# One order written out for all five engines, and three full-array visits of TensorE in a head pair

## The chip, the cores and the metric

The kernel runs on one core of a Trainium2 chip. The metric is the device time of one execution in microseconds. The engines are TensorE (PE; its weight loads are shown as PEld), VectorE (DVE), ScalarE (ACT), GpSimd (POOL) and the DMA queues, most of which SyncE (SP) issues.

## What is computed

The reference is sparse attention over key chunks, and a mixture of experts that sends each token to one expert:

```python
ub = sum(max(q * k_min_of_chunk, q * k_max_of_chunk))     # 24 chunks of 32 keys
top_chunks = argsort(where(causal, ub, -1e9))[..., -6:]
scores = scale * q @ k.T, masked to chosen chunks and to the past
attn = softmax(scores) @ v                                # 4 batches x 8 heads x 768 x 64
x = attn as 3072 tokens x 512
logits = x @ w_gate; expert = argmax(logits)              # 8 experts
out = gate * relu(x @ w1[expert]) @ w2[expert]
```

Inputs are float32; the seed of the draw is fixed.

## The kernel before

Two heads make a head pair; there are 16 pairs, `i` from 0 to 15, four to a batch (`hp = i % 4`). One pair is taken through its stages while parts of its neighbours are worked on in between: `n = i + 1` is prepared for attention, `m = i + 2` has its keys and queries transposed, `i - 1` gets its denominators and router logits, `i - 2` the last of its output rows.

The stages of a pair, with the names used below:

- k0, k1 (`k_half`): three fp32 transposes of keys each into a PSUM buffer, on DVE the maximum and minimum of each chunk (L207, L208), on ACT two scaled bf16 copies into KTE (L209, L210). q0, q1: the same for queries; DVE copies to qT (L224), ACT writes the absolute value to qA and one head's bf16 copy to QSB (L225, L227). The other head's bf16 copy of qT is made by POOL (L226); it is put into the list `late` and issued when `flush()` is called. `flush()` first empties the list `sums_` (POOL additions of router logits, L375 and L378), then `late`.
- `kse` (L233, L234): sums and differences of the chunk extremes, on DVE. `ub`: bounds by matmuls of 64 columns, evicted by ACT as ubT (L244). `select`: transposes (L249), and on DVE ubm, twelve max8 and nsel (L251, L259, L262). `mask`: nsel transposed, 64 columns wide, and copied by ACT into rows 64 to 87 of QSB (L271, L272), so that unselected chunks get a large negative score in the score matmul.
- `scores(i, u)` for seven units `u`: 0 and 1 are the first 384 queries, 2 to 6 the last 384; each is 768 score columns over the two heads (L298), an exp on ACT into P (L303), and where keys reach the diagonal a causal mask on POOL (`affine_select`, L307; one for units 0 and 5, two for 1 and 6). Units 1 and 6 consist of two parts of 256 and 128 queries, each with an exp of its own.
- `attend(i, u)`: P times V in 64-column halves, one head in each (AV, L320); after units 1 and 6 DVE copies the sum out (ot, L325); the P tiles of a query half are added up on DVE (L332) for the denominators.
- `router_steps`: `ud` multiplies the added-up P with a column of ones and the output with the gate weights, 32 columns wide (L348, L353), evicted by ACT (L356); `lgp` transposes it and divides (L361, L363, L367); `x0`, `x1` transpose the output and scale it into rows of x (L386, L388).
- `route_steps`, once per batch: `logits` and exp, `rank` (matmuls L432 to L438, then DVE), and six scatters of rows to DRAM by POOL (L454).

PSUM has three buffers for transposes and the like (`ps_m`, bufs=3), two for scores (`ps_s`), one for AV (`ps_o`). A buffer is handed on when its readers are done.

The pair loop has four groups, g0 to g3. Each runs its scores, then pieces of the neighbours' work, then `attend` for the units (0, 1), (2, 3), (4, 5), (6). The order in which PE, POOL and SP issue is the order of the program text:

```python
with tc.manual_schedule(engines={PE, POOL, SP}):
```

For DVE and ACT, a planner chooses the order from its own estimates, except in the first pair's start and from pair 15 on. On PE the order within a pair is: scores 2, 3, x1, AV 0, 1, ub (g0); scores 4, 5, rank, select, AV 2, 3, ud (g1); scores 6, k0, mask, AV 4, 5 (g2); lgp, x0, the next pair's scores 0, 1, k1, q0, q1, AV 6 (g3). Matmuls of 128 columns use the full array; AV, ub and mask are 64 columns wide, ud is 32. `flush()` is called in g0, after ub.

After the loop the last denominators and the routing of the last batch are interleaved with the first expert tiles (`up`, `down`), whose rows POOL gathers and DMA transposes (`gather`, `x_in`); the gathers of the first tiles are issued at the beginning of pair 15. A table of what each tile holds is computed by DVE in three steps during pairs 13 and 14 (`early_table`).

Of the kernel before, what the change touches and what calls it, by code (L numbers as in the profile page):

```python
# [24 lines left out]
def kernel(  # L25
# [74 lines left out]
    KS = [buf.tile([128, 64], FP32, name=f"KS{i}") for i in range(2)]  # L100
    KD = [buf.tile([128, 64], FP32, name=f"KD{i}") for i in range(2)]
# [6 lines left out]
    def consts_first():  # L108
# [12 lines left out]
        nc.gpsimd.memset(KS[0][:], 0.0)  # L121
        nc.gpsimd.memset(KD[0][:], 0.0)
# [15 lines left out]
    def consts_last():  # L138
        nc.gpsimd.memset(KS[1][:], 0.0)
        nc.gpsimd.memset(KD[1][:], 0.0)  # L140
# [7 lines left out]
        nc.sync.dma_start(out=wgb[64:128, :, E:2 * E], in_=wg_v[64:128])  # L148
        iota(rev8[:], [[-1, E]], base=E)
# [44 lines left out]
    def prep_steps(i):  # L194
        s = st[i]
        kte, qsb, ks, kd = KTE[i % 2], QSB[i % 2], KS[i % 2], KD[i % 2]
        kmx = {}

        def k_half(hf):
# [3 lines left out]
            pt = ps_m.tile([128, 384], FP32, tag="m")  # L203
            for t in range(3):
                nc.tensor.transpose(pt[:, ts(t, 128)], s["k"][:, 3 * hf + t], ident_f[:])
            pk = pt[:].rearrange("p (c w) -> p c w", w=CH)
            nc.vector.tensor_reduce(s["kmx"][:, ts(hf, 12)], pk, AX.X, ALU.max)  # L207
            nc.vector.tensor_reduce(s["kmn"][:, ts(hf, 12)], pk, AX.X, ALU.min)  # L208
            nc.scalar.activation(kte[0:64, 0, ts(hf, 384)], pt[0:64, :], AF.Copy, bias=0.0, scale=0.125)  # L209
            nc.scalar.activation(kte[0:64, 1, ts(hf, 384)], pt[64:128, :], AF.Copy, bias=0.0, scale=0.125)  # L210

        def q_t(hf):
            pt = ps_m.tile([128, 384], FP32, tag="m")
            for t in range(3):
                nc.tensor.transpose(pt[:, ts(t, 128)], s["q"][:, 3 * hf + t], ident_f[:])
            s[f"qp{hf}"] = pt

        def q_e(hf):
            pt = s[f"qp{hf}"]
            if hf == 0:  # L220
                s["qT"] = work.tile([128, 2, 384], FP32, tag="qT", name="qT")
                s["qA"] = work.tile([128, 2, 384], FP32, tag="qA", name="qA")
            qT, qA = s["qT"], s["qA"]
            nc.vector.tensor_copy(out=qT[:, hf], in_=pt[:])  # L224
            nc.scalar.activation(qA[:, hf], pt[:], AF.Abs)  # L225
            late.append(lambda: nc.gpsimd.tensor_copy(out=qsb[0:64, 0, ts(hf, 384)], in_=qT[0:64, hf]))  # L226
            nc.scalar.activation(qsb[0:64, 1, ts(hf, 384)], pt[64:128, :], AF.Copy)  # L227

        def kse():
            for hd in range(2):  # L230
                r = slice(64 * hd, 64 * hd + 64)
                c = slice(32 * hd, 32 * hd + NCH)
                nc.vector.tensor_tensor(ks[r, c], s["kmx"][r, :], s["kmn"][r, :], ALU.add)  # L233
                nc.vector.tensor_tensor(kd[r, c], s["kmx"][r, :], s["kmn"][r, :], ALU.subtract)  # L234

        def ub():
            pu = ps_m.tile([128, 384], FP32, tag="m")
            for w_, nm in ((ks, "qT"), (kd, "qA")):
                x_ = s[nm][:].rearrange("p a c -> p (a c)")
                for h in range(2):  # L240
                    nc.tensor.matmul(pu[64 * h:64 * h + 64, 0:320], lhsT=w_[:], rhs=x_[:, ds(128 + 320 * h, 320)],
                                     start=(nm == "qT"), stop=(nm == "qA"), skip_group_check=True)
            s["ubT"] = work.tile([128, 384], FP32, tag="ud", name="ubT")
            nc.scalar.activation(s["ubT"][:, 0:320], pu[:, 0:320], AF.Copy)  # L244

        def select():
            pt = ps_m.tile([128, 3, 2, 2, 32], FP32, tag="m")
            for t in range(3):
                nc.tensor.transpose(pt[:, t], s["ubT"][:, ds(c0s[t], 128)], ident_f[:])  # L249
            ubm = work.tile([128, 3, 2, 2, NCH], FP32, tag="ubm")  # L250
# [14 lines left out]
        def mask():  # L265
            pt = ps_m.tile([64, S], BF16, tag="m")
            for hf in range(2):
                for t in range(3):
                    nc.tensor.transpose(pt[:, ds(128 + 320 * hf + c0s[t], 128)],
                                        nsel[:, t, hf].rearrange("p a n -> p (a n)"), ident_b[:])  # L270
            nc.scalar.activation(qsb[64:64 + NCH, 0, 128:S], pt[0:NCH, 128:S], AF.Copy)  # L271
            nc.scalar.activation(qsb[64:64 + NCH, 1, 128:S], pt[32:32 + NCH, 128:S], AF.Copy)  # L272

        return dict(k0=lambda: k_half(0), k1=lambda: k_half(1), q0=lambda: q_t(0),
                    q1=lambda: q_t(1), q0e=lambda: q_e(0), q1e=lambda: q_e(1), kse=kse, ub=ub, select=select, mask=mask)


# [4 lines left out]
    def scores(i, u):  # L282
        kte, qsb = KTE[i % 2], QSB[i % 2]
        qb, parts = units[u]
        ps = ps_s.tile([128, 2, 512], FP32, tag="s", name="ps")
        if u in (0, 2):
            P = work.tile([128, 2, 384], FP32, tag="Pa", bufs=4, name="Pa")
        else:
            P = work.tile([128, 2, 384], FP32, tag="Pr", bufs=4, name="Pr")
        st[i][f"P{u}"] = P  # L290
        pvs = []
        for n, (kb, w, c0) in enumerate(parts):
            if len(parts) == 1:
                pv = ps[:, :, 0:w]
            else:
                pv = ps[:, n, 0:2 * w].rearrange("p (a w) -> p a w", a=2)
            for hd in range(2):
                nc.tensor.matmul(pv[:, hd, :], lhsT=kte[:, hd, ts(kb, 128)],  # L298
                                 rhs=qsb[:, hd, ds(qb * 384 + 384 - w, w)],
                                 start=True, stop=True, skip_group_check=True)  # L300
            pvs.append(pv)
# [572 lines left out]
```

## Time and profile before

| | us |
|---|---|
| three runs, median (lowest to highest) | 360.99 (360.24 to 362.16) |
| the profiled execution | 360.64 |
| its span, first to last instruction | 358.6 |
| attention, up to the last ud eviction | 248.8 |
| a plain head pair | 13.66 |

The pair's length is the distance of successive ACT evictions of ubT or ud in the timeline (for example 122.27 and 135.92). The granted TensorE clock is 0.992 of full speed over the span. In the profile, L12 is line 12 of the kernel; "a <- b" with a time in brackets is idle time before an instruction and what released it. The busy time of PE includes the modelled ends of pipelined matmuls, so a short wait can be hidden in it.

### The profile page before, as it was taken

Reading aid. Unit: us, or ns where it says so; the run is one execution under the profiler, and the core shown is the slowest. Engines: PE = TensorE matmul, PEld = TensorE weight load, DVE = VectorE, ACT = ScalarE, POOL = GpSimd, SP = SyncE. Lnnn points to the kernel's source line nnn. Section 1 sums busy time; section 2 is a strip of 40 time slices with the busy share of each in tenths; the row PEclk is TensorE's granted clock in tenths of the full one; section 3 lists DMA queues with packets and bytes.
Section 4 is the critical chain, followed back from the end, with each engine's and each line's share of the span. In section 5 each row is a group of like instructions: output and inputs, shape, how many; then the busy total and the mean of one; then the engine's idle time right before and its main releaser. Section 6 shows DMA issues by size and latency. Waiting matters only on the chain. (4 is left out here: it accounts for less than half of the span.)

```text
span 358.6 us, 7585 instructions
## 1 busy us (share of the span) xinstructions
PE 326.9 (91%) x2312; PEld 171.5 (48%) x2312; DVE 235.0 (66%) x815; ACT 231.2 (64%) x398; POOL 180.4 (50%) x296
## 2 busy tenths in 40 slices
PE   6679999999899999999999988998799999999990
PEld 5535455455455465554554545443344344444430
DVE  5799889889999898999988999846460000000000
ACT  2497797797687897867977967642344444445440
POOL 3075425445474453466534547575577665653331
PEclk9999999999999999999999999999999999999996
DMA  8619998999957999937989973476999999998851
GB/s 153 112 26 194 210 220 139 215 167 215 207 127 151 182 176 195 202 100 178 200 134 212 187 148 113 73 135 116 165 211 233 221 237 197 203 186 201 157 126 48
DMA packets 138215, 59.83 MB, mean 167 GB/s; under 512 B 122811, under 2 KB 131005, under 8 KB 138176
## 3 DMA queue, kind: packets, MB, share of 16 engines
q1 hardware_dynamic: 119072, 29.52, 45.4%
q0 software_dynamic: 17536, 29.42, 42.0%
q10 hardware_dynamic: 1568, 0.39, 0.6%
q8 instruction: 21, 0.34, 0.4%
q14 instruction: 18, 0.15, 0.2%
HBM read 56.14 MB, written 10.51 MB: 186 GB/s over the span
## 5 line engine op out<-in xcount | busy, mean ns | idle before, releaser
L332 DVE TENSOR_TENSOR Pa<-Pa,Pr 128x768 f32<-128x768 f32 (+2 forms) x112 | 81.6, 729 | 1.1
L307 POOL TENSOR_SCALAR_AFFINE_SELECT Pr<-Pr 128x256 f32<-128x256 f32 x80 | 33.5, 437 | 67.3 <-ACT Pr L303 66.1
L303 ACT ACTIVATE Pr<-ps 128x768 f32<-128x768 f32 (+2 forms) x112 | 65.0, 630 | 3.2 <-PE ps L298 2.9
L612 PE MATMUL py<-w_all,hT 128*128 x224 | 52.7, 379 | 2.7 <-DMA hT<-h__3653 1.9
L298 PE MATMUL ps<-QSB,KTE 128*128 128x384 bf16 (+2 forms) x288 | 50.4, 292 | 1.2 <-DVE QSB L711 0.2
L620 POOL DMA_INDIRECT out_dram<-y,ti_all x28 | 27.8, 993 | 30.2 <-ACT y L619 26.3
L298 PEld LDWEIGHTS <-KTE 128*128 128x128 bf16 x288 | 24.1, 97 | 27.3 <-issue 21.2
L612 PEld LDWEIGHTS <-hT 128*128 128x128 bf16 x224 | 21.8, 98 | 29.5 <-DMA hT<-h__3653 2.3
L619 ACT ACTIVATE y<-py,gt_all 128x512 f32<-128x512 f32 x27 | 18.6, 687 | 20.8 <-PE py L612 18.4
L454 POOL DMA_INDIRECT xs_dram<-xrow,sli x24 | 26.9, 1121 | 7.7 <-issue 5.0
L356 ACT ACTIVATE ud<-pu 128x384 f32<-128x384 f32 x16 | 7.9, 492 | 32.8 <-PE pu L353 30.7
L303 ACT ACTIVATE Pa<-ps 128x768 f32<-128x768 f32 x32 | 26.0, 812 | 3.8 <-PE ps L298 3.2
L601 PE MATMUL ph<-w_all,KTE 128*128 x120 | 28.4, 379 | 0.0
L169 POOL DMA_DIRECT2D w_all<-in_moe_w_dram x32 | 24.3, 760 | 0.0
L307 POOL TENSOR_SCALAR_AFFINE_SELECT Pa<-Pa 128x256 f32<-128x256 f32 x16 | 6.4, 398 | 35.3 <-ACT Pa L303 35.3
L601 PE MATMUL ph<-w_all,QSB 128*128 x96 | 22.7, 379 | 0.3 <-issue 0.3
L575 DVE TENSOR_TENSOR ti_all<-xgqA,inv_i 128x1 int32<-128x1 int32 x9 | 1.4, 159 | 29.6 <-DMA xgqA<-xs_dram,grow 29.6
L554 POOL DMA_INDIRECT xgqA<-xs_dram,grow x14 | 14.6, 1046 | 10.2 <-issue 3.3
L554 POOL DMA_INDIRECT xgqT<-xs_dram,grow x14 | 14.5, 1033 | 8.7 <-DVE gt_all L577 4.9
L325 DVE COPY ot<-po 128x384 f32<-128x384 f32 x32 | 17.7, 553 | 1.6 <-PE po L320 0.9
L575 DVE TENSOR_TENSOR ti_all<-xgqT,inv_i 128x1 int32<-128x1 int32 x8 | 1.3, 159 | 26.5 <-DMA xgqT<-xs_dram,grow 26.5
L226 POOL CAST QSB<-qT 64x384 bf16<-64x384 f32 x30 | 16.3, 551 | 4.1 <-DVE qT L224 2.8
(311 smaller groups left out, 665.0 us busy)
## 6 DMA issues: line engine op xcount, KB each, us to landing
w_all<-in_moe_w_dram POOLq DMA_DIRECT2D x32, 512.0 KB, 6.0
out_dram<-y,ti_all POOLq DMA_INDIRECT x28, 3.6
t__122<-in_k_dram SPq DMA_DIRECT2D x2, 192.0 KB, 3.5
t__125<-in_q_dram ACTq DMA_DIRECT2D x2, 192.0 KB, 4.0
t__128<-in_v_dram SPq DMA_DIRECT2D x2, 192.0 KB
t__196<-in_k_dram SPq DMA_DIRECT2D x2, 192.0 KB, 3.1
t__206<-in_q_dram SPq DMA_DIRECT2D x2, 192.0 KB, 3.8
t__209<-in_v_dram SPq DMA_DIRECT2D x2, 192.0 KB
```

Source lines behind the costliest of these rows:

```text
L169: nc.gpsimd.dma_start(out=dst, in_=src.rearrange("(c p) f -> p c f", p=128))
L298: nc.tensor.matmul(pv[:, hd, :], lhsT=kte[:, hd, ts(kb, 128)], rhs=qsb[:, hd, ds(qb * 384 + 384 - w, w)], start=True, stop=True, skip_grou ...
L303: nc.scalar.activation(P[:, :, ds(c0, w)], pv, AF.Exp)
L307: nc.gpsimd.affine_select(out=pd, in_=pd, pattern=[[0, 2], [1, 128]], compare_op=ALU.is_ge, fill=0.0, base=0, channel_multiplier=-1)
L325: nc.vector.tensor_copy(out=ot[:], in_=po[:])
L332: nc.vector.tensor_tensor(acc[:, :, 384 - w:384], acc[:, :, 384 - w:384], P[:, :, ds(c0, w)], ALU.add)
L454: d = nc.gpsimd.indirect_dma_start(out=xs_dram[:], out_offset=bass.IndirectOffsetOnAxis(ap=sli[:, u:u + 1], axis=0), in_=bst[b][f"xrow{u % ...
L554: d = nc.gpsimd.indirect_dma_start(out=xg_bufs[j % XB].bitcast(I32), out_offset=None, in_=xs_dram[:], in_offset=bass.IndirectOffsetOnAxis( ...
L601: nc.tensor.matmul(ph[:, fh, :], lhsT=xT[:, c, :], rhs=w_all[:, ds(wo + (c * F + fh * 512), 512)], start=(c == 0), stop=(c == NDC - 1), sk ...
L612: nc.tensor.matmul(py[:], lhsT=hT[:, c, :], rhs=w_all[:, ds(wo + (W1W + c * DM), DM)], start=(c == 0), stop=(c == NFC - 1))
L619: nc.scalar.activation(y[:], py[:], AF.Copy, bias=0.0, scale=fs[j]["gt"])
L620: d = nc.gpsimd.indirect_dma_start(out=out[:], out_offset=bass.IndirectOffsetOnAxis(ap=fs[j]["ti"], axis=0), in_=y[:], in_offset=None, bou ...
```

## The change

- DVE and ACT too are put in the order of the program text, everywhere. For this each helper is cut into a PE part, a DVE part and an ACT part (`k_mm`, `k_v`, `k_a`; `q_mm`, `q_v`, `q_a`; `ub`, `ub_a`; `sel_mm`, `sel_v`; `mask`, `mask_a`; `ud`, `ud_a`; `lgp_mm`, `lgp_v`; `x_mm`, `x_v`; `rank_mm`, `rank_v`; `logits`, `expo`, `gates`). `attend` becomes `av`, `add` and `o_ev`, `scores` becomes `scores` and `exps`.
- Unit 6's scores are issued at the end of g1, ahead of `ud`, as matmuls of 64 columns: two halves of the keys for each head and part. k0 moves from g2 to g1, behind the selection transposes (in pair 0 it stays in g2). On PE the order becomes: scores 2, 3, x1, AV 0, 1, ub; scores 4, 5, selection, k0, rank, AV 2, 3, scores 6, ud, mask, AV 4, 5; lgp, x0, next scores 0, 1, k1, q0, q1, AV 6.
- Units 1 and 6 keep the two heads in two PSUM banks, and one exp takes both parts.
- The additions of P tiles 5 and 6 are issued in the next pair's g0, behind `kse` of this one.
- `kse` works on both heads together: one sum, one difference, and one product with a 0/1 mask `bm`.
- `flush()` moves from g0 to g1, behind `ud_a`.
- `logits` moves from the end of g3 of the pair with hp = 0 into g0 of the pair behind it, `expo` and `gates` follow in g1; the scatters are spread otherwise. Constants that only routing needs are made in pair 2 (`consts_route`).

```diff
-    KS = [buf.tile([128, 64], FP32, name=f"KS{i}") for i in range(2)]
-    KD = [buf.tile([128, 64], FP32, name=f"KD{i}") for i in range(2)]
+    KSD = [buf.tile([128, 2, 2, 32], FP32, name=f"KSD{i}") for i in range(2)]
+    bm = buf.tile([128, 2, NCH], BF16, name="bm")
...
+        def kse():
+            kt2 = work.tile([128, 2, NCH], FP32, tag="top8", name="kt2")
+            nc.vector.tensor_tensor(kt2[:, 0], s["kmx"][:], s["kmn"][:], ALU.add)
+            nc.vector.tensor_tensor(kt2[:, 1], s["kmx"][:], s["kmn"][:], ALU.subtract)
+            nc.vector.tensor_tensor(ksd[:, :, :, 0:NCH], kt2[:].unsqueeze(2).to_broadcast([128, 2, 2, NCH]),
+                                    bm[:].unsqueeze(1).to_broadcast([128, 2, 2, NCH]), ALU.mult)
...
+    def scores(i, u, split=False):
...
+        n = 64 if split else 128
+        for kb, w, c0 in parts:
+            for hd in range(2):
+                for h in range(128 // n):
+                    nc.tensor.matmul(ps[ds(h * n, n), hd, ds(c0, w)], lhsT=kte[:, hd, ds(kb * 128 + h * n, n)],
+                                     rhs=qsb[:, hd, ds(qb * 384 + 384 - w, w)],
+                                     start=True, stop=True, skip_group_check=True)
...
+        nc.scalar.activation(P[:], ps[:, :, 0:384], AF.Exp)
...
-    spread = ((), (0,), (2, 4), (1,), (3, 5), (), (), ())
+    spread = ((), (), (0, 2, 4), (), (1, 3), (5,), (), ())
...
+    with tc.manual_schedule(engines={PE, POOL, SP, DVE, ACT}):
...
             for g in range(4):
                 if g == 0:
-                    scores(i, 2)
-                    scores(i, 3)
-                    run(rout, i - 2, "x1")
+                    for u in (2, 3):
+                        scores(i, u)
+                        exps(i, u)
+                    run(rout, i - 2, "x_mm", 1)
+                    run(rout, i - 2, "x_v", 1)
+                    if i > 0:
+                        if n < NP:
+                            add(i - 1, 5)
+                        add(i - 1, 6)
+                    av(i, 0)
+                    av(i, 1)
+                    o_ev(i, 0)
+                    if router:
+                        logits()
+                    add(i, 1)
+                    run(prep, n, "ub")
+                    run(prep, n, "ub_a")
+                    if 0 < i < NP - 1:
+                        load(n, "v")
                 elif g == 1:
...
+                    for u in (4, 5):
+                        scores(i, u)
+                        exps(i, u)
+                    run(prep, n, "sel_mm")
+                    if i > 0:
+                        run(prep, m, "k_mm", 0)
+                        run(prep, m, "k_a", 0)
+                    if router:
+                        rank_mm()
+                    run(prep, n, "sel_v")
+                    if router:
+                        expo()
+                        rank_v()
+                        gates()
+                    if i > 0:
+                        run(prep, m, "k_v", 0)
+                    av(i, 2)
+                    av(i, 3)
+                    add(i, 3)
+                    scores(i, 6, True)
+                    exps(i, 6)
+                    run(rout, i - 1, "ud")
+                    run(rout, i - 1, "ud_a")
+                    flush()
                 elif g == 2:
-                    scores(i, 6)
...
+                    run(prep, n, "mask")
+                    run(prep, n, "mask_a")
...
+                    av(i, 4)
+                    av(i, 5)
+                    add(i, 4)
+                    if m >= NP:
+                        add(i, 5)
                 else:
...
+                    run(rout, i - 1, "lgp_mm")
+                    run(rout, i - 1, "x_mm", 0)
+                    if n < NP:
+                        for u in (0, 1):
+                            scores(n, u)
+                            exps(n, u)
+                    run(rout, i - 1, "lgp_v")
+                    run(rout, i - 1, "x_v", 0)
+                    run(prep, m, "k_mm", 1)
+                    run(prep, m, "k_v", 1)
+                    run(prep, m, "k_a", 1)
+                    for hf in range(2):
+                        run(prep, m, "q_mm", hf)
+                        run(prep, m, "q_v", hf)
+                        run(prep, m, "q_a", hf)
                     if i + 3 < NP:
                         load(i + 3, "k", "q")
...
+                    av(i, 6)
+                    o_ev(i, 1)
+                    run(prep, m, "kse")
+                    if hp == 0 and b > 0:
+                        flush(sums_)
...
-                if g == 0:
-                    run(prep, i + 1, "ub")
-                    flush()
...
+                if 4 * i + g == 10:
+                    consts_route()
```

## The prediction

> **What bounds the kernel now.** First the page, for the stages: the engines' busy times and the slices of the span (tenths, 9 us each).
>
> ```profile
> PE 326.9 (91%) x2312; PEld 171.5 (48%) x2312; DVE 235.0 (66%) x815; ACT 231.2 (64%) x398; POOL 180.4 (50%) x296
> ...
> PE   6679999999899999999999988998799999999990
> ...
> DVE  5799889889999898999988999846460000000000
> ```
>
> DVE ends after slice 29: up to about 250 us the attention runs, with PE and DVE both near nine tenths. The expert stage (250 to 358.6) is not edited. Next the windows, cut at successive ubT evictions, one per head pair: a plain pair, then one with routing.
>
> ```profile
> 122.27:135.92 13.65, 13.57 (x109) 7.45 (x108) 12.61 (x39) 11.35 (x22) 6.30 (x13) 1.00 0.99 165
> 149.72:165.35 15.63, 14.21 (x119) 7.72 (x119) 14.93 (x53) 11.39 (x22) 9.90 (x15) 1.00 0.66 153
> ```
>
> Columns after the length: busy us of PE, weight loads, DVE, ACT, POOL. In a plain pair PE has no gap (13.57 of 13.65), DVE has 1.0 us, ACT 2.3, POOL half. In the routing pair DVE is full too. Last the timeline of one plain pair (110 to 126 us), for what holds PE inside that busy time and when POOL works.
>
> ```profile
> 112.42 0.95 DVE L332 TENSOR_TENSOR Pa<-Pa,Pr 128x768 f32<-128x768 f32 x1
> ...
> 113.29 0.55 DVE L207 TENSOR_REDUCE kmx<-pt 128x12 f32<-128x384 f32 x1
> 113.37 0.76 POOL L307 TENSOR_SCALAR_AFFINE_SELECT Pr<-Pr 128x256 f32<-128x256 f32 x2 [1.59 <-ACT Pr L303]
> ...
> 117.81 0.48 ACT L209 ACTIVATE KTE<-pt 64x384 bf16<-64x384 f32 x1 [0.21 <-DVE kmn L208]
> ...
> 118.92 0.70 POOL L226 CAST QSB<-qT 64x384 bf16<-64x384 f32 x1
> ...
> 121.56 0.81 ACT L303 ACTIVATE Pr<-ps 128x768 f32<-128x768 f32 x1
> ...
> 122.42 0.10 PEld L298 LDWEIGHTS <-KTE 128*128 128x128 bf16 x1 [0.30 <-issue]
> ...
> 122.75 0.31 PEld L249 LDWEIGHTS pt<-ident_f,ubT 128*128 128x128 f32 x3 [0.23 <-ACT ubT L244]
> ```
>
> Three things. (a) Unit 5's scores wait until the exp of unit 3 (121.56 to 122.37) frees its score buffer, and the selection transposes behind them start at 122.75 when ubT is there: 0.27 us of PE waiting in each pair, hidden in pipelined busy time. (b) That exp is late because ACT's chain of k copies, q copies and exps starts at 117.81, when the DVE minimum of the same PSUM bank is done. (c) The causal masks of unit 6 run beside reductions from PSUM, and the bf16 copies of qT (L226) run at 118.92, 10 us before the next unit-0 scores (129.1) read them.
>
> And one view from elsewhere, what POOL does when adds come in a row:
>
> ```profile
> 228.11 2.83 DVE L332 TENSOR_TENSOR Pa<-Pa,Pr 128x768 f32<-128x768 f32 x3
> ```
> ```profile
> 228.53 1.87 POOL L307 TENSOR_SCALAR_AFFINE_SELECT Pr<-Pr 128x256 f32<-128x256 f32 x2 [1.60 <-ACT Pr L303]
> ```
>
> Two masks took 1.87 us where the two at 113.37 took 0.76: each ended only about 0.27 us after the add that it met.
>
> **What the Trainium skill says.** "TensorEngine Tiling (Array Packing)", section Key Properties: a change of tiling mode drains TensorE. The trace agrees: three fp32 transposes take 0.35 us, and from selection to AV it is 0.48, so 0.13 for the change; from AV6 to the next scores 0.16. "PSUM — Partial Sum Buffer", section PSUM bank collisions: two engines may not read one bank at once. Here ACT did start 0.09 after kmn's end, with the data there for 1.2 us. "SBUF — State Buffer", section Who interferes with whom: a DVE instruction with two SBUF inputs contends with GpSimd's reads, the other blocks for the whole instruction. The 1.87 us agree. "TensorE: Matmul & The Clock Gate", section Weight-path perf modes: fast weight load wants 128 columns; no row here times bf16 scores with 64 columns.
>
> **The change part by part.** Times are from the start of LGP (lgp_mm's transposes) in a plain pair; before it is 114.63.
>
> *The visit removed.* Before: k0's transposes stand between UD (32 columns) and mask (64 columns), four full-array visits, nine changes of mode in a pair. After: three visits, eight changes. Before, selection to next LGP: 0.48 + 1.44 (AV2, AV3) + 1.11 (UD) + 0.34 (scores 6) + 0.43 (k0) + 1.74 (mask, AV4, AV5) = 5.54. After: 0.35 + 0.48 (k0 with its change) + 1.28 + x + 0.16 + 1.11 + 1.74 = 5.12 + x, x being unit 6 in 64-column halves. Bounds of x: 0.32 (768 columns in pairs side by side, as fp32 AV does) and 0.45 (eight loads of about 0.055, the spacing of the mask's transposes). I take 0.40: 5.52. The visit is worth 0.02 (-0.05 to +0.08).
>
> *ACT's chain to selection.* e1 is one activation, ending at 2.91 rather than 2.97, but the k copies still wait for kmn: kmx follows lgp_v and x_v without the 512 add between, 2.02 rather than 2.07. So 3.13 for 3.18. qa1 now precedes e2; two swapped items leave e3 where it was (6.93 to 6.88), so selection comes at 8.07 for 8.12. e2 ends at 6.98, just ahead of scores 4 (7.16). Gain 0.05. A plain pair without new waits: 8.07 + 5.52 = 13.59 against 13.66.
>
> *DVE.* kse from four small instructions and gaps (119.64 to 120.52, 0.88) to three, estimated 0.6. Adds 5 and 6 of the pair before (0.86 + 0.95) move behind x_v into g0; o_ev(0) then starts 7.17, add 1 ends 8.5, and selection's DVE work is ready to start at 8.65: nothing lost, and mask has 1.1 us of cover. If that cover went, mask waits for nsel. k_v(0) follows nsel at 10.74, so adds 3 and 4 come back to back from 11.67 to 13.4; LGP's DVE work is due at 14.19.
>
> *k0 earlier* (8.42 for 11.49): its load is issued at 2.0, and its last packet is about 5.7 after LGP, landing below 7.5 in every pair by the DMA records; the SP queue's order is the same. Nothing.
>
> *POOL, the step that decides.* flush() moves from g0 to behind unit 6's masks. POOL's order becomes mask 6 (two), sums (0, 1 or 2), two qT copies. Scores 6 start at 10.18, e6 runs 10.78 to 11.59, so the first mask issues at 11.66, with add 3 at 11.67. POOL alone: 0.77 + two sums 0.86 + first copy 0.50 = 2.13, at 13.79; scores 0 of the next pair, due at 13.59 + 0.79 = 14.38, would not see it. But two 768 adds (0.86 each) hold the port in that window; each lets a POOL operation out 0.27 after its end: mask 12.85, mask 13.85, sums 14.65, copy 15.15. Scores 0 wait until 15.2, 0.84 late; k1, ACT's chain and all else follow scores 0, so the pair is longer by that. With one sum 0.45, with none nothing. Bounds for two sums: 0 (POOL always first) and 1.3.
>
> Queued behind the waiting scores on PE: unit 1, k1, q0, q1, AV6; ACT and DVE wait for all of them.
>
> Sums: pair 2 has one; 3, 4, 7, 8, 11, 12 two; 6, 10, 14 one; 1, 5, 9, 13 none. Against 13.66: two sums +0.77, one +0.38, none -0.07.
>
> *Routing pairs (5, 9, 13 and the one behind).* Logits move into g0 ahead of add 1. The dependent run takes 1.42 in the tail of this trace (254.63 to 256.05), rank's 0.95, gates 0.71. Rank waits 0.36 on PE and works 0.30; mask waits for rank's PSUM buffer, 0.5: LGP 1.18 late. DVE's backlog makes k_v(1) 0.57 late, and x_v(1) waits for the row buffer that scatters 0, 2, 4 free, 0.4 to 0.6. About 2.2 over two pairs; before, 97.53 to 125.97 less two plain pairs costs 1.1 and 82.89 to 97.53 another 1.0: 2.1. Equal; pair 10 was 0.3 longer before. In 13/14 the expert table's steps (1.35, 1.0, 1.4 as dependent runs) stand in line where they were interleaved: +0.5. Bounds: -1 to +2 each.
>
> *Constants.* About 1.35 us of DVE work leaves the start (24.07 to 25.6, where o_ev is late and AV2 waits 0.42): -0.3, as k's load bounds the next step at 28.6. It reappears behind add 4 in pair 2: +0.3.
>
> *Tail.* The gathers of pair 15 and their DMAs (233.72 to the first down projection, 255.04, where PE waits 1.86) set it; add 6 behind x_v costs DVE 0.46 inside that wait. Nothing.
>
> Sum: start -0.3; pair 1 -0.1; pair 2 +0.7; six pairs of two sums +4.6; pairs 6 and 10 +0.8; routing +0.1, -0.2, +0.5. Together +6.1.
>
> The profiled execution took 360.64 (span 358.6 and 2.0 around it), 0.35 below the median 360.99. 360.64 + 6.1 = 366.7; against the median it would be 367.1.
>
> **Rivals.**
> *R1, copies in time.* POOL gets the port between the adds, or e6 comes 0.8 earlier. For it: POOL needs only 2.13 of 2.7 us. Against: 228.53. Then +6.1 loses 5.9 (6 x 0.84 + 2 x 0.45): 360.8.
> *R2, ACT's chain comes forward: faster.* If the k copies start with e1's end (2.81) and not after kmn, scores 5 and selection lose the wait of (a): selection at 7.77, 0.35 per pair; with the copies in time, thirteen pairs x 0.35 off R1: 356. It decides from 0.3 us of earlier start. Against: the 0.21 us wait at 117.81, and k_v still precedes k_a.
> *R3, DVE's backlog.* Should mask get k0's PSUM buffer instead of rank's, it waits for k_v(0), 14.6 rather than 13.0: 1.7 in each of three pairs, 372. For it: three buffers turn in order. Against: at 218.27 q1 waits for lgt, thus took the buffer freed last, not the next in turn.
>
> **How the numbers follow.** Forecast 0.53, own range 363.5 to 369.5; R1 0.20; R2 0.15; R3 0.12. Half a per cent, 1.8 us, is what a measurement here can tell from no change. Faster: R2 and a little of R1, 0.17. Same: most of R1, 0.19. Slower: the rest, 0.64. The range 358.8 to 370.8 takes in R1, the low edge leaving R2 out and the high edge most of R3.
>
> **What would show it.** A plain two-sum pair of 14.4 us with scores 0 released by POOL's copy (L226's successor), and pairs 5 and 9 free of that wait; selection at 8.0 to 8.1 after LGP; unit 6's halves within 0.32 to 0.45. Plain pairs of 13.6 make R1 right; of 13.2, R2; a mask that waits above 1 us for k_v, R3. A stall on x_v longer than 1 us, or k0 waiting for its load, would be a thing I missed.

## The result and the profile after

The changed kernel takes 422.12 us (median of 4 runs, 421.94 to 428.24) against 361.11 (360.24 to 362.16) for the kernel before on the same chip: a ratio of 1.172, 95% interval 1.163 to 1.182. The profiled execution took 428.24 us with a span of 426.5. Some executions below were disturbed and ran slower; ratios leave them out (of e8 one of four stays, so it has no interval), and the traces of e2, e8 and e14 are of disturbed executions.

The page of the changed kernel, parts 1 and 2: busy time by engine, then busy tenths and granted clock in 40 slices.

```profile
PE 345.7 (81%) x2376; PEld 182.8 (43%) x2376; DVE 240.4 (56%) x799; ACT 230.5 (54%) x366; POOL 183.5 (43%) x297
...
PE   6688968496858859695989949496978999999990
...
PEclk9999969598969897888899979799999999999997
```

TensorE has holes in most slices of the attention part, where before it had hardly any, and in the slices with holes its granted clock falls as well (mean 0.918; 0.992 before). The loss is all there: from the first to the last LGP the pairs take 273.6 us (45.1 to 318.7) where they took 206.1 (44.2 to 250.3). What lies ahead and behind is within 1 us of before.

The waits by engine and line of the changed kernel (total us, times, longest us), and one row of its DMA part (32 loads of 512 KB, median us from issue to landing; 6.0 before):

```profile
ACT KTE L218 <- PE pk L207: 44.2, 10, 5.8
PEld pk L207 <- issue: 41.8, 9, 5.9
...
DVE kmx L212 <- ACT KTE L218: 24.0, 7, 5.1
```
```profile
w_all<-in_moe_w_dram POOLq DMA_DIRECT2D x32, 512.0 KB, 8.2
```

L207 is k0's and k1's transposes. TensorE's weight load for them waits 41.8 us in 9 places, and 44.2 us of ACT are spent waiting for them. "Issue" means that no engine released them. What did is in the timeline of one pair of the changed kernel, from LGP at 146.3 on (start, duration, engine and line; in brackets the idle time before it and what ended it):

```profile
148.14 1.61 POOL L172 DMA_DIRECT2D w_all<-in_moe_w_dram  x2
148.21 1.05 SPq L193 DMA_DIRECT2D t__1823<-in_k_dram  x2
...
159.55 0.87 PE L207 MATMUL pk<-ident_f,t__1823 128*128 128x128 f32 x3 [4.72 <-DMA t__1823<-in_k_dram]
...
160.46 0.98 ACT L218 ACTIVATE KTE<-pk 64x384 bf16<-64x384 f32 x2 [4.83 <-PE pk L207]
...
163.91 0.81 ACT L325 ACTIVATE Pr<-ps 128x768 f32<-128x768 f32 x1 [2.47 <-issue]
164.79 0.76 POOL L329 TENSOR_SCALAR_AFFINE_SELECT Pr<-Pr 128x256 f32<-128x256 f32 x2 [8.68 <-ACT Pr L325]
...
167.21 1.43 POOL L172 DMA_DIRECT2D w_all<-in_moe_w_dram  x2
```

Two loads of the experts' weights (w_all, 512 KB each) are issued at 148.14, together with the load of the keys. The keys land 10.8 us after their issue; before they took 3.0 to 4.9 in every pair for which the DMA view gives a time. k0 stands in g1 now and wants them at 154.8: it waits 4.72 us, and AV 2 and 3, unit 6 and the denominators stand behind it on TensorE, unit 6's exponential behind k0's copies on ACT. So unit 6's masks are late on POOL (8.68 us of idle time), and behind these masks stand `flush()` and the next two weight loads. They go out at 167.21, once more beside the next load of keys (169.1). The lateness of one pair isn't needed for that of the next: the pair from LGP at 224.02 to LGP at 237.72 waits for no keys and takes 13.70 us, and yet the next two weight loads go out at 239.72, 0.83 us ahead of the keys, which land after 11.5 us. The place of the loads in POOL's order was enough there.

In the kernel before, the weight loads of one pair's end and the keys went out like this:

```profile
110.97 0.81 POOL L169 DMA_DIRECT2D w_all<-in_moe_w_dram  x1
...
114.08 0.79 POOL L169 DMA_DIRECT2D w_all<-in_moe_w_dram  x1
...
116.63 0.96 SPq L190 DMA_DIRECT2D t__1811<-in_k_dram  x2
```

There g1's loads stood behind unit 5's masks, and unit 6 was in g2, so the two loads were 3.1 us apart and the last of them 2.6 us ahead of the keys.

### The profile page after: what moved, and what is told of

Its sections match the earlier page's. It is cut to its first block, busy times and chain, and to the rows that moved or that the text cites. A ratio compares the mean times of both kernels' runs of the same rounds, so it can differ in the third digit from the quotient of the medians.

```text
span 426.5 us, 7566 instructions
## 1 busy us (share of the span) xinstructions
PE 345.7 (81%) x2376; PEld 182.8 (43%) x2376; DVE 240.4 (56%) x799; ACT 230.5 (54%) x366; POOL 183.5 (43%) x297
## 5 line engine op out<-in xcount | busy, mean ns | idle before, releaser
L325 ACT ACTIVATE Pr<-ps 128x768 f32<-128x768 f32 x80 | 63.5, 816 | 34.0 <-issue 14.3
L218 ACT ACTIVATE KTE<-pk 64x384 bf16<-64x384 f32 x60 | 29.1, 485 | 50.0 <-PE pk L207 44.2
L311 PE MATMUL ps<-QSB,KTE 128*128 128x384 bf16 (+4 forms) x352 | 52.6, 302 | 2.3 <-POOL QSB L243 0.8
L311 PEld LDWEIGHTS <-KTE 128*128 128x128 bf16 (+1 forms) x352 | 28.5, 113 | 33.5 <-issue 26.9
L212 DVE TENSOR_REDUCE kmx<-pk 128x12 f32<-128x384 f32 x32 | 17.8, 555 | 31.4 <-ACT KTE L218 24.0
L325 ACT ACTIVATE Pa<-ps 128x768 f32<-128x768 f32 x32 | 26.0, 812 | 15.1 <-PE ps L311 14.6
L494 POOL DMA_INDIRECT xs_dram<-xrow,sli x24 | 24.6, 1027 | 6.1 <-issue 5.3
L293 ACT ACTIVATE QSB<-pm 24x640 bf16<-24x640 bf16 x30 | 20.8, 693 | 5.8 <-PE pm L287 5.3
L421 DVE TENSOR_TENSOR xrow<-px,rec 128x384 bf16<-128x384 f32 x32 | 17.5, 550 | 6.7 <-DMA xs_dram<-xrow,sli 5.2
L594 POOL DMA_INDIRECT xgqA<-xs_dram,grow x14 | 14.6, 1042 | 14.2 <-DMA KTE<-xgqA 4.5
L370 PE MATMUL pu<-Pa,dcol 128*32 128x384 f32 x128 | 18.2, 625 | 0.3 <-DVE Pa L350 0.3
L641 PEld LDWEIGHTS <-KTE 128*128 128x128 bf16 x120 | 11.7, 98 | 15.8 <-DMA KTE<-xgqT 1.4
```

Source lines behind the costliest of these rows:

```text
L218: nc.scalar.activation(kte[0:64, hd, ts(hf, 384)], pt[64 * hd:64 * hd + 64, :], AF.Copy, bias=0.0, scale=0.125)
L293: nc.scalar.activation(qsb[64:64 + NCH, hd, 128:S], s["pm"][32 * hd:32 * hd + NCH, 128:S], AF.Copy)
L311: nc.tensor.matmul(ps[ds(h * n, n), hd, ds(c0, w)], lhsT=kte[:, hd, ds(kb * 128 + h * n, n)], rhs=qsb[:, hd, ds(qb * 384 + 384 - w, w)], s ...
L325: nc.scalar.activation(P[:], ps[:, :, 0:384], AF.Exp)
L494: d = nc.gpsimd.indirect_dma_start(out=xs_dram[:], out_offset=bass.IndirectOffsetOnAxis(ap=sli[:, u:u + 1], axis=0), in_=bst[b][f"xrow{u % ...
L641: nc.tensor.matmul(ph[:, fh, :], lhsT=xT[:, c, :], rhs=w_all[:, ds(wo + (c * F + fh * 512), 512)], start=(c == 0), stop=(c == NDC - 1), sk ...
```

## The experiments

Fourteen kernels ran. Each is compared with the kernel before on its own chip, which took 368 to 369 us on the two chips of e1 to e8 and 360 to 361 on those of the others, so ratios are given. "W" below is the theory that weight loads beside an early load of keys make the loss, "F" the forecast's (POOL's late copies), "H" that the written order of DVE and ACT itself costs it.

### POOL's queue taken apart (e1, e2, e4) and k0 back in g2 (e3)

```diff
# e1: flush() back at the end of g0
                     run(prep, n, "ub_a")
+                    flush()
...
                     run(rout, i - 1, "ud_a")
-                    flush()
# e2: the weight loads of g1 ahead of unit 6 (left out of the general loop below for g = 1)
                     for u in (4, 5):
                         scores(i, u)
                         exps(i, u)
+                    for w in range(NW):
+                        if wq[w] == 4 * i + g:
+                            load_w(w)
# e3: k0 in g2 in every pair
-                    if i > 0:
-                        run(prep, m, "k_mm", 0)
-                        run(prep, m, "k_a", 0)
...
-                    if i == 0:
-                        run(prep, m, "k_mm", 0)
+                    run(prep, m, "k_mm", 0)
# e4: the edits of e1 and e2
```

> flush() back at the end of g0, all else as after the change. Theory W (a burst of weight loads runs beside the k load, and k0, now 3 us earlier on TensorE, waits for that load): the weights of g1 still stand behind unit 6's masks on POOL and so still run into those of g2, so most of the loss stays: 395 to 418 us, k0 waiting 3 us or more in most pairs. Theory F (the forecast's: copies and sums behind unit 6's masks, under DVE's adds, hold up scores 0): about 6 us come back, 414 to 418 us, with k0's waits unchanged. Theory H (the hand order of ACT and DVE itself, k0's copies ahead of unit 6's exponential and the routing in line, is what costs): no change, 420 to 425 us.

> Only the weight loads of g1 move: issued right behind unit 5's score masks, ahead of unit 6, flush() and the loads of g2. Theory W: the burst is broken, the k load lands 4 to 6 us after its issue rather than 10 to 12, k0 waits less than 0.5 us in a plain pair, and the granted clock comes back above 0.97: 362 to 376 us. Theory F: no change beyond 2 us, 420 us. Theory H: no change beyond 5 us, 417 to 422 us.

> k0 (transposes, copies and reductions) goes to g2 behind unit 6, as pair 0 has it: the fourth full-array visit is back and the weight loads stay where the change put them. Theory W: k is wanted 3 us later, and what stood behind the waiting k0 (AV 2 and 3, unit 6, its exponential, the masks, flush and the weight loads) runs on time, so that the burst itself comes earlier: 362 to 380 us, k0 waiting under 1 us. If the burst alone delays the load by 6 us and k0's place is unimportant, 395 us or more. Theory F: 420 us. Theory H with k0's copies ahead of the exponential as the cost: the same 362 to 380 as W; with routing and the adds as the cost, above 405.

> flush() at the end of g0 and the weight loads of g1 ahead of unit 6: POOL's queue in the order that it had before the change, with the three visits and the hand order of DVE and ACT kept. Theory W: 360 to 370 us, and the difference from the kernel with the weight loads moved alone is what theory F is worth by itself, 0 to 7 us. Theory F alone: 414 to 418. Theory H: above 405 us.

| kernel | median us | ratio to before | 95% interval | ratio x 361.1 |
|---|---|---|---|---|
| changed kernel | 422.12 | 1.172 | 1.163 to 1.182 | 423.3 |
| e1, flush() in g0 | 394.76 | 1.069 | 1.059 to 1.078 | 385.9 |
| e2, weights ahead of unit 6 | 387.34 | 1.043 | 1.032 to 1.053 | 376.5 |
| e3, k0 in g2 | 390.25 | 1.058 | 1.051 to 1.066 | 382.1 |
| e4, e1 and e2 | 375.83 | 1.021 | 1.014 to 1.028 | 368.6 |

Each edit alone brings back more than half of the loss, so the parts don't add: 37 us for `flush()`, 47 for the weights, 41 for k0's place, 55 for the first two together. F alone is out: it gave 6 us for e1 and about nothing for e2 and e3. H, read as the whole loss, is out: e4 keeps the whole written order of DVE and ACT. W is borne out in kind, but its sizes were off. It expected 395 us or more of e1, which took less: `flush()` stood between the masks and the weight loads, so putting it back lets these go out earlier too, and the waits of k0's transposes for their load fall from 43.5 us to 17.8. It expected 362 to 380 us of e3, with k0 waiting under 1 us, and e3 took more: k0 still waits 3.1, 2.2 and 2.2 us in three pairs. For e2 (362 to 376) and e4 (360 to 370) the last column comes out at the edge and within, the times themselves above.

With the weights ahead, `flush()` alone is worth e2 less e4, 0.022 or 8 us (3 to 12 by the two intervals). That is near the 6 us of the forecast, but e12 below shows that only a part of it is the wait that the forecast described.

### The same two parts in the kernel before (e6, e7, e8), and DVE and ACT given back (e5)

```diff
# e6: the kernel before with the three visits
                     run(prep, i + 1, "select")
+                    if i > 0:
+                        run(prep, i + 2, "k0")
                 elif g == 2:
-                    scores(i, 6)
...
                 if g == 1:
+                    scores(i, 6, True)
                     run(rout, i - 1, "ud")
#     and g1's weight loads behind unit 5's masks, as they were
# e7: the kernel before, g1's weight loads moved to the end of g2
-                    if wq[n] == 4 * i + g:
+                    if g == 2 and wq[n] in (4 * i + 1, 4 * i + 2) or g in (0, 3) and wq[n] == 4 * i + g:
# e8: e6, with g1's weight loads left at the end of g1, behind unit 6's masks
# e5: e4, DVE and ACT in the planner's order outside the first pair and the tail
-    with tc.manual_schedule(engines={PE, POOL, SP, DVE, ACT}):
+    with tc.manual_schedule(engines={PE, POOL, SP}):
```

> The kernel of e4 (three visits; flush() and the weight loads of g1 in POOL's old order) with DVE and ACT given back to the planner outside the first pair and the tail. The kernel of e4 stood 2.1% above before; its trace lays about 3.6 us of that on the expert table's DVE steps standing in line in pairs 13 and 14 and about 1.2 us on each of three routing pairs. Theory H (the hand order of DVE and ACT is that rest): ratio 0.985 to 1.005 to before. Theory V (the visits or the split unit 6 cost it): the ratio stays at 1.015 to 1.025. If the planner does worse in plain pairs, 1.02 or more with plain pairs longer than the 13.4 us of e4.

> The kernel before with the visits alone: k0 moved to stand with selection, unit 6 in 64-column halves ahead of the denominators, g1's weight loads issued behind unit 5's masks as they were; flush() in g0 and DVE and ACT left to the planner. Theory W: the k load lands in time, so the ratio to before is 0.985 to 1.01 (the visit was put at 0.02 us a pair; e4's plain pairs of 13.4 to 13.5 us point to 0.2). If k0's early place costs by itself, without a burst: 1.03 or more, with k0 waiting over 1 us in most pairs.

> The kernel before with one thing changed: the weight loads of g1 are issued at the end of g2, right before those of g2 and so right before the next k load; k0 stays where it was, 11.5 us behind LGP. Theory W (burst and early k0 together make the loss): the k load lands 9 to 12 us after its issue, at 11 to 14 us behind LGP, and k0 waits 0 to 2 us: ratio 1.00 to 1.06. If the burst alone makes the loss: 1.12 or more. If the burst is harmless and k0's place is all: below 1.005, k landing in 4 to 5 us.

> The visits of e6 in the kernel before, with g1's weight loads left at the end of g1 and so behind unit 6's masks: early k0 and burst together, without the hand order and without flush() moved. Theory W: most of the loss of the change is here, ratio 1.07 to 1.17, k0 waiting 3 to 6 us in most pairs and TensorE's clock at half speed behind each such wait. Theory F and H, in which flush() or the hand order make the loss: below 1.03. (The kernel with flush() put back stood at 1.07 with the hand order.)

| in the kernel before | k0 where it was | k0 early, three visits |
|---|---|---|
| weight loads apart | 1 | e6: 1.016 (1.007 to 1.025) |
| weight loads together | e7: 1.004 (0.999 to 1.008) | e8: 1.065 (one run) |

e8's ratio is of one run only, 392.07 us over 368. The four cells speak for W without any written order of DVE and ACT: the burst alone costs nothing that can be told (in e7's trace k0 waits for its keys only at the start, 0.6 us, as before), early k0 and the halves of unit 6 cost 1.6%, and both together about 6.5%. In e8's trace TensorE waits for k0's keys in eleven pairs, 18.9 us in all and up to 5.9. In e7 the two weight loads still go out about 2.5 us ahead of the keys (115.11 and 117.66), in most pairs of e8 about 2 to 3 us ahead.

The 1.6% of e6 are more than W gave it (1.01 at most), and waits for keys don't make them: k0 waits 0.2 and 0.3 us, in two pairs. Its plain pairs are 13.9 us long instead of 13.66; why the planner's order does worse there was not found.

e5 stands at 1.032 (1.022 to 1.041), so the planner's order for DVE and ACT is no better than the written one as a whole, and H fails for the rest of e4 too. It is mixed in detail: e5's plain pairs take 13.9 to 14.2 us (e4's 13.5), its pairs 13 and 14 together 28.3 (e4's 30.1).

### Where the weights stand, and what is left of the forecast's own mechanism (e12)

```diff
-                    if wq[w] == 4 * i + g:
+                    if g == 3 and wq[w] in (4 * i + 1, 4 * i + 2) or g == 0 and wq[w] == 4 * i:
```

> The changed kernel, flush() where the change put it, with the weight loads of g1 and g2 still issued together, two in a row, but behind the k and q loads of g3 and not ahead of them. Theory W says that it is the weights ahead of the k load that delay it: k lands 4 to 6 us after its issue, k0 waits under 1 us in a plain pair, ratio 1.02 to 1.06 (the copies of flush() alone stood at about 11 us between e2 and e4). If two weight loads together delay k wherever they stand, k0 waits 3 us or more and the ratio is 1.10 or more.

e12 took 376.87 us, a ratio of 1.047 (1.038 to 1.056). The weight loads of g1 and g2 are still issued two in a row, but behind the keys and queries. The keys now land 3.2 to 4.2 us after their issue, by e12's DMA view (two rows of it; the weights wait instead, 9.3 us in the median):

```profile
t__1363<-in_k_dram SPq DMA_DIRECT2D x2, 192.0 KB, 4.1
...
t__1616<-in_k_dram SPq DMA_DIRECT2D x2, 192.0 KB, 3.8
```

k0 doesn't wait in any pair of its trace after the first. So it is what stands ahead of the keys that delays them, not how the weights are grouped. (The changed kernel has one such case itself: at 226.72 its two loads went out 0.8 us behind the keys, and these landed in 3.9 us.) Moving two DMA issues by a few us takes 45 us off (1.172 to 1.047), and e12 still has `flush()` where the change put it. It is therefore the kernel in which the forecast's mechanism can be seen without the waits for keys. Its timeline, around the LGP at 135.7 of a pair with two sums:

```profile
133.90 1.49 POOL L329 TENSOR_SCALAR_AFFINE_SELECT Pr<-Pr 128x256 f32<-128x256 f32 x2 [1.78 <-ACT Pr L325]
...
134.17 2.02 DVE L350 TENSOR_TENSOR Pa<-Pa,Pr 128x768 f32<-128x768 f32 x2
...
135.36 1.55 POOL L407 TENSOR_TENSOR lg<-lg,lgt 128x96 f32<-128x96 f32 x2
...
136.85 0.94 POOL L243 CAST QSB<-qT 64x384 bf16<-64x384 f32 x2
...
137.40 0.82 PE L311 MATMUL ps<-QSB,KTE 128*128 128x384 bf16 x6 [0.81 <-POOL QSB L243]
```

Two masks take 1.49 us beside DVE's adds instead of 0.76, the sums 1.55, the first bf16 copy of qT ends about 137.3, and scores 0 have waited 0.81 us for it. The waits say 5.1 us in 7 places for scores on that copy: about 0.8 in each of five pairs with two sums, 0.7 in the sixth, and 0.3 in pair 2. Plain pairs with two sums are 14.2 to 14.4 us long, those with none or one 13.6 to 13.7. In the other three two-sum pairs (4, 8 and 12, each from its LGP to the next, which takes in a rank of routing) the wait is there, but they are only 0.1, 0.1 and 0.7 us longer than in e4.

The largest single loss of e12 against e4 lies elsewhere, in pair 2 (17.5 us, in e4 14.1):

```profile
61.43 0.29 DVE L159 TENSOR_SCALAR U<-colf,iota_p 128x128 bf16<-128x128 f32 x1 [2.01 <-POOL colf L105]
...
62.96 0.22 DVE L392 RECIPROCAL rec<-pl 128x12 f32<-128x12 f32 x1
...
63.74 1.51 PE L234 MATMUL pq<-ident_f,t__749 128*128 128x128 f32 x6 [2.43 <-issue]
```

POOL makes the constants for routing behind the moved sums and copies. DVE, in written order, waits 2.01 us for them with LGP's reciprocal behind that wait, and q's transposes, which come once LGP's work is done, wait 2.43 us.

### The rest of e4: the routing pairs (e9), the visit (e11), the table (e10, e13, e14)

```diff
# e9: e4, with the routing logits and the scatters as before the change
-                    if router:
-                        logits()
...
                         flush(sums_)
+                        route[b - 1][0]()
...
-    spread = ((), (), (0, 2, 4), (), (1, 3), (5,), (), ())
+    spread = ((), (0,), (2, 4), (1,), (3, 5), (), (), ())
# e10: e9, the expert table's three steps one quarter later each
-                if 4 * i + g in (4 * NP - 10, 4 * NP - 9, 4 * NP - 8):
+                if 4 * i + g in (4 * NP - 9, 4 * NP - 8, 4 * NP - 7):
# e13: e9, the three steps at 4 * NP - 7, - 6 and - 5
# e14: e13, gates() behind add(i, 3)
# e11: e4, with k0 and unit 6 (128 columns) in g2 behind the denominators
```

> The kernel of e4 (ratio 1.021 to before) with the routing pairs mended: the routing logits back at the end of the pair ahead, and the scatters of a batch's rows spread (0), (2, 4), (1), (3, 5) as before the change rather than (0, 2, 4), (1, 3), (5). In e4 rank waits 1.17 us on TensorE for the one-hot, and three scatters in a row on POOL hold the masks of the next pair 1 us. If these are part of what is left: 3 to 6 us off, ratio 1.005 to 1.013, with the pairs of 15.1, 15.1 and 19.2 us shorter by 1 us or more. If what is left lies in the plain pairs or in the k load: no change, 1.018 to 1.024.

> As e9, and the expert table's three steps on DVE one quarter of a pair later each, the first behind the k reductions and the q copies of pair 13's last quarter rather than ahead of LGP's DVE work. In e4 that pair took 19.2 us against 15.6. If the table's place is the cause: another 2 to 4 us off, ratio 0.995 to 1.007. If the wait there is for weights, gathers or the nsel of selection: within 1 us of e9.

> The kernel of e4 with the fourth full-array visit back: k0 and unit 6, with 128 columns, in g2 behind the denominators as before the change, in the same hand order otherwise. The forecast put the visit at 0.02 us a pair (-0.05 to +0.08): then a plain pair of 13.4 to 13.5 us and a ratio within 0.005 of e4's 1.021. If the visit is worth 0.2 us a pair, plain pairs of 13.6 us and 3 us more, less what k0's later place saves in waits (2.6 us in e4).

> The kernel of e9 (ratio 1.010 to before) with the expert table's three steps on DVE at the ends of pair 14's second to last quarters, where no keys or queries are prepared, instead of pairs 13 and 14 around LGP. If the table in line with LGP's DVE work is what makes pair 13 19.7 us long (15.6 before): that pair falls to 15.5 to 17 us, ratio 0.997 to 1.003. If the scatters on POOL or the backlog from rank and gates make it: 18 us or more, ratio 1.006 to 1.012. If the gathers of pair 15 then wait for the table, the tail is longer than 107 to 108 us by what the pair gained.

> As e13, and the routing gates on DVE behind the reductions of k0 and add 3 rather than ahead of them. In e9 the pair after each rank takes 15.3 us against 13.9 before, LGP's DVE work starting 1 us late behind rank, gates, reductions and adds in line. If the gates' place decides: 0.3 to 0.9 us off each of three pairs, ratio 0.992 to 1.0, a version about level with before or just faster. If the row buffers' scatters decide (they wait for the gates): no gain, or 1 us worse.

| kernel | median us | ratio to before | 95% interval | pairs 13 and 14, us |
|---|---|---|---|---|
| before (first profile) | 361.11 | 1 | | 15.6 + 11.1 |
| e4 | 375.83 | 1.021 | 1.014 to 1.028 | 19.2 + 10.9 |
| e9, routing as before | 365.44 | 1.010 | 1.003 to 1.017 | 19.6 + 11.2 |
| e10, table a quarter later | 367.56 | 1.018 | 1.011 to 1.025 | 17.8 + 12.6 |
| e13, table in pair 14 | 365.78 | 1.017 | 1.012 to 1.022 | 15.2 + 15.6 |
| e14, and gates later | 376.46 | 1.045 | 1.040 to 1.050 | |
| e11, four visits | 370.45 | 1.026 | 1.019 to 1.033 | 18.1 + 10.9 |

By the ratios e9 gives 3.7 us back, as was expected, but the intervals of e4 and e9 overlap, and the pairs of the two traces differ by 1.4 us in sum. Nor is it in the pairs named: the routing pairs fall from 15.9, 15.8 and 15.6 to 15.4, and pairs 10 and 11 from 14.5 and 14.3 to 13.7, while the two of 15.1 stay (15.3; 13.9 before). The largest lot left lies in pairs 13 and 14, 30.8 us where they took 26.7. The timeline of e9 shows how (LGP at 219.7):

```profile
222.46 0.82 DVE L526 CAST nt<-nt_i 128x8 f32<-128x8 int32 x1
...
223.31 0.38 DVE L530 TENSOR_TENSOR tmp<-tri,nt 128x64 f32<-128x64 f32 x1
...
223.86 0.22 DVE L392 RECIPROCAL rec<-pl 128x12 f32<-128x12 f32 x1
...
224.64 1.51 PE L234 MATMUL pq<-ident_f,t__3082 128*128 128x128 f32 x6 [3.05 <-issue]
```

The table's short operations (L521 to L532) stand in line ahead of LGP's reciprocal, that holds LGP's PSUM buffer, and q's transposes wait 3.05 us for a buffer. But the theory of its place fell: in e13 pair 13 is 15.2 us long and pair 14 grew from 11.2 to 15.6. In three places tried, pairs 13 and 14 take about 4 us more than before, and the excess moves with the table; in the planner's order of before its small pieces were interleaved. A place that is free was not found. e14 missed by far: AV waits for DVE to copy the last sum out, up to 3.5 us at a time in its trace. None of the fourteen was faster than the kernel before.

e11 gives the visit its price within the written order. From selection to the next LGP it takes 5.75 us (80.39 to 86.14), e4 5.51, the kernel before 5.54, and e11's plain pairs are 13.7 us long where e4's are 13.5. (The total times, 1.026 and 1.021, don't separate the two.) e4's plain pair, of 13.48 us, is this one:

```profile
73.36 0.55 PE L386 MATMUL pl<-ident_f,ud 128*128 128x128 f32 x3
...
81.33 0.55 PE L263 MATMUL pt<-ident_f,ubT 128*128 128x128 f32 x3
...
83.47 0.50 PE L311 MATMUL ps<-QSB,KTE 128*64 128x256 bf16 x8
...
83.90 0.85 PE L370 MATMUL pu<-Pa,dcol 128*32 128x384 f32 x8
...
86.84 0.55 PE L386 MATMUL pl<-ident_f,ud 128*128 128x128 f32 x3
```

Selection stands 7.97 us behind LGP and unit 6 in halves takes 0.43 (83.47 to 83.90).

## Why the prediction was wrong

The direction was right, the size was not: 366.7 us forecast, 422.12 measured. The direction is only in small part to the forecast's credit: the wait that it described measures 5.1 us of some 62, and the rest comes from terms that it put at nothing or nearly so. Point by point:

- *The visit removed* (0.02 us a pair, unit 6 at 0.40): right against the kernel before. Selection to LGP was put at 5.52 and is 5.51 in e4; unit 6 in halves 0.43. Within the written order the fourth visit costs 0.24 (e11), more than the 0.08 at which the forecast bounded it.
- *ACT's chain* (selection at 8.07, a plain pair of 13.59): right in kind, 7.97 and 13.48.
- *k0 earlier* is the step that failed: "its load is issued at 2.0, and its last packet is about 5.7 after LGP, landing below 7.5 in every pair by the DMA records; the SP queue's order is the same. Nothing." The numbers were true of the kernel before. SP's order did stay the same, but the landing time depends on the load and on all that is in flight beside it, and that is set by POOL, whose weight loads stood behind the very steps that were moved. The step should have had a term for the k load beside 1 MB of weights: about 11 us after its issue at 2, that is 13 behind LGP against 8.4, a wait near 5 us in each pair that has two such loads. Measured: 41.8 us in 9 places. The forecast had a warning in its own window of a plain pair: the numbers behind POOL's column, which it left unread, are the clock (1.00), the DMA share (0.99) and GB/s (165), so the DMA engines were busy nearly all the time already. It did name the sign, "k0 waiting for its load, would be a thing I missed".
- *POOL, the step that decides*, named the right move and listed POOL's order as "mask 6 (two), sums (0, 1 or 2), two qT copies". The list ended too early: behind the copies come the weight loads. The wait that was in the list was sized well: scores 0 late by 0.84 in a pair with two sums, 0.81 in e12; a plain two-sum pair of 14.4, 14.2 to 14.4. R1 put all such waits at 5.9 (with the third one-sum pair of its own sum it would be 6.4), measured 5.1; of the one-sum pairs only pair 2 shows any, 0.3. That the move costs 8 us without the burst (e2 to e4) comes near the forecast's 6.1 partly by luck, since constants that POOL makes late, which had no such term, take 3.4 of it in pair 2 of e12.
- *Routing and the table*: put at about +0.4 together. Going back to the old places of logits and scatters is worth 3.7 us by ratios and 1.4 by traces (e9), the two pairs behind rank keep 1.3 each, and the table adds 4 where +0.5 stood. The terms were made from dependent runs of short instructions, and left out that these hold back LGP's reciprocal and with it a PSUM buffer.
- *Constants, start, tail*: with `flush()` in g0 the constants' pair is 14.1 against 13.7 (+0.5, put at +0.3), with `flush()` in g1 17.5. The start, up to the first LGP, is 0.9 longer in the changed kernel where -0.3 stood; the tail is equal within 0.5.

The sum of the loss, in ratios times 361.1: 62 us; of these 45 for the weights ahead of the keys (to e12), 9.5 for `flush()` behind unit 6 and what goes with it (e12 to e4; 5.1 of waits for the copies, of which some are hidden, and 3.4 in pair 2), 3.7 for routing (e4 to e9, weakly shown), and 3.8 left in e9. e9's trace is of the longest of its executions and spans 7.4 us more than the first profile: pairs 13 and 14 have 4.1 more than before, the two pairs behind rank 1.3 each and the start 2.7, less about 2 that other pairs and the tail save.

Of the rivals none came. R3 wanted the mask to wait above 1 us for k0's buffer; in e4's routing pairs it waits 0.6 to 0.7, and for nsel or an eviction (1.9 in pair 13, for nsel). R2 wanted selection 0.3 us earlier than the forecast, and it came 0.1 earlier. R1 was refuted by the 0.81 us in e12.

Only 41.8 of the 67.9 us between the two spans are k0's waits. TensorE is also busy 13.6 us longer than in e4 with the same matmuls (345.7 against 332.1), as it runs slower behind a wait. The windows of the changed kernel around the wait shown above (length; busy time and count of PE, PEld, DVE, ACT, POOL; clock; DMA share; GB/s):

```profile
146.30:154.83 8.53, 8.45 (x65) 5.12 (x63) 7.56 (x18) 7.28 (x14) 4.41 (x8) 1.00 0.69 104
154.83:159.55 4.72, 0.00 (x1) 0.04 (x1) 2.50 (x16) 0.80 (x2) 0.41 (x1) 0.86 1.23 218
159.55:165.80 6.25, 6.25 (x42) 2.84 (x44) 2.85 (x4) 1.91 (x4) 1.01 (x3) 0.56 0.44 74
165.80:167.20 1.40, 1.40 (x12) 0.55 (x9) 0.00 (x0) 1.35 (x3) 1.32 (x4) 1.00 0.00 0
```

After 4.72 us without work the clock is down, and the next 6.25 us run at 0.56 of full speed. At full speed the same work would take about 3.5 (6.25 x 0.56; e4 takes 3.6 from k0 to AV 4, 81.71 to 85.35), so a wait of 4.7 us costs about 7.4, an estimate from these windows. The second line also shows the cause at work: the DMA engines are fully taken and move 218 GB/s. The Trainium skill, "TensorE: Matmul & The Clock Gate", section Part 1: The HAM clock gate, says that the array falls to half its clock after an idle window of about 3.4 us; the trace agrees, since by windows of 0.5 us the clock fell at about 158.2, 3.4 us into the wait. It says that a busy window of about 3.4 us brings it back, and that the windows are free-running; here full clock came back at about 165.0, 5.5 us after the work had begun again, more than one such window and less than two.

## What to carry to other kernels

When a step is moved, write down everything behind it in each in-order queue that it moves through, down to the DMA issues: here two weight loads behind two moved copies cost 45 us, the waits for the copies 5.1. A landing time read from a trace holds only for the transfers in flight beside it; a consumer that is moved earlier must be checked against the load in its new company, and a bulk load with no deadline belongs behind the load that is waited for (e12: 45 us for one line). And where an order is written out for an engine that is nearly full, look at what stands behind short chains such as a router or a table: here the table cost about 4 us in each of three places.

## What the runs showed of the hardware

- A load of keys, 2 x 192 KB on SP's queue, lands in 3.0 to 4.9 us in the kernel before, and in 8.8 to 13.0 us in the nine pairs of the changed kernel with the long waits, where two loads of 512 KB from POOL's queue went out up to 2.3 us ahead of it, though the queues are two. With two loads behind it, it took 3.2 to 4.2 us (e12). The Trainium skill, "DMA: Bandwidth & Descriptors", section Issuing engines are not separate DMA queues, says that transfers of all issuing engines run on the same DMA engines and interleave. The trace agrees, and the size follows: 1.05 MB of weights and 0.79 MB of keys and queries at 218 GB/s are 8.4 us, an estimate from the window above.
- Issuing took long as well: beside the weight loads (DMA share 0.95 from 149.37 to 153.80) the two issues of q's load held SP's queue for 4.42 us at 149.37, where two of k's took 1.05.
- TensorE's half clock outlasted the wait that caused it: from about 158.2 to 165.0 around a wait that ended at 159.55. The two pairs in a row that had no wait for keys ran in 15.0 and 13.7 us at a clock of 1.00.
